# Unread products, own tiles for the first V tails, a later pair of norms and two moves to VectorE, in a kernel of two interleaved attention layers

## The chip, the cores and the metric

The kernel runs on one core of a Trainium2 chip. The metric is the time of one execution on the device, in microseconds. Every kernel is run several times, and the median counts. One execution was also recorded by the hardware profiler; all views quoted here are of that execution. A core has five engines that work side by side: TensorE (PE in the profile; its weight loads are PEld), VectorE (DVE), ScalarE (ACT), GpSimd (POOL) and SyncE (SP), which here only issues transfers. "SPq" and "ACTq" are the issues of transfers by SP and ACT.

## What is computed

Two layers, A and B, are run as A, B, A, B on a sequence of 2048 tokens of width 640. Each adds its result to its input, and each normalises its input first:

```python
x = A_x
x = x + _A_ref(_layernorm(x), ...)
x = x + _B_ref(_layernorm(x), ...)
x = x + _A_ref(_layernorm(x), ...)
x = x + _B_ref(_layernorm(x), ...)
```

Layer A has 32 heads of width 20 and cuts the sequence into 4 segments of 512. Within a segment it is causal softmax attention; it is mixed with a linear attention to a state (M, z) that has summed phi(k) v and phi(k) of the segments before. Layer B has 32 heads of width 128 and goes through 64 segments of 32 tokens one after the other. In each, 8 memory rows and the 32 tokens attend to each other, and the first 8 rows of the result are the memory of the next segment:

```python
for s in range(n_seg):
    h = concatenate([mem, x[s*32:(s+1)*32]])
    q, k, v = h @ Wq, h @ Wk, h @ Wv          # 32 heads of 128
    p = softmax(q k^T * scale, masked)
    o = (p v) @ Wo
    mem = o[:8];  outs.append(o[8:])
```

Inputs, weights and the output are bfloat16.

## The kernel before

**Layer A** (`layer_A`) takes 32 groups of 4 heads in one segment each, 8 per segment, and two more passes of its loop to drain. The first segment's four blocks of 128 rows are loaded, normalised (`seg_norm`) and transposed (`seg_tr`) ahead of the loop; then come the projections of the first group: `proj_q` (tile a_QP), two `proj_kv` (a_KV) and `k_turn` (a_KT). In the loop, `s_mask` puts the causal mask into PSUM by a product of the identity with c_negu, `s_mm` adds the scores (a_S), and `s_max` takes the negative row maxima on VectorE. `q_with_max` adds these maxima to the queries (a_Q), and the copy a_q of that is what the second round of scores needs: `t_round` (a_T) writes transposed scores, three rounds for each pair of heads, `t_exp` applies the exponential on ACT into a_PT, and an affine_select on POOL clears the part above the diagonal. `pv` (a_PV) multiplies with the values, `norm` divides. The pipeline is deep: group g's maxima are taken in pass g, its T rounds come one and a half passes later, its `pv` two passes later. `filler` places one group's projections and copies between the rounds.

After the last pass `last_turns` transposes the normalised rows of the last segment (a_otps), `last_oT` copies them, and `out_stage_b` multiplies them with the output weights (a_YP, two halves of 320 columns for each of four blocks of 128 rows), adds the input on VectorE (a_xnew), stores the sum (xres), makes a bfloat16 copy on ACT (a_xnb, one buffer) and stores that too (xres_bf).

The order of TensorE is the order of the program text. ACT, VectorE and POOL in A are put in order by `KeyOrder`, which sorts instructions by a due time: the step's number plus a lag from `A_LAGS`. SP's order, and all that carries no such rule, is left to the scheduler of the build. PSUM in A is in two pools: three tiles of two banks (psx, for a_S and a_T) and two of one bank (pg, for all else). A tile taken from a pool waits until its predecessor in that buffer was read.

**Layer B** (`layer_B`) is one chain: step s needs the memory rows that step s-1 gave. To keep TensorE's tiles full, what doesn't depend on the memory is computed ahead. Groups of 128 rows are normalised (`ln_norm`, `layernorm_tile`) and transposed (`ln_spread`); the first 24 tokens of each segment go to HX, beside the 8 memory rows, and the last 8 ("tails") of eight segments are gathered in TX. `tail_unit` and `tail_evac` project the tails to queries and keys in 8 units and store them to DRAM (QKd); `vtail_unit` and `vtail_evac` do so with the values in 8 units and store them to VTd. Each step loads its own tails back: `tails_load` (b_tl), `tails_copy`, `vtails_in` (b_Vth).

Ahead of step 0 stand, in the program's text: the loads and norms of four groups, with two spreads; the 8 tail units of the first eight segments, of which the odd k are evicted on VectorE and the even on ACT; the first projections (b_Kp, b_Qp) and their transposes; the loads of the output weights b_wo on SP; the load of the first tails; the 8 V-tail units, evicted by VectorE (even k) and ACT (odd k), stored through SP (even) and ACT (odd); the V rows of the first segment (b_V); `vtails_in(0)`; and one unit of the next eight segments. Each of these evictions needs a place in SBUF. `vt_homes` gives the V tails' places:

```python
vt_homes = [(wk, x) for x in ("vt", "E0", "msb", "PTa", "PTb", "OTsb", "vt", "E0")]
```

so units 6 and 7 write where units 0 and 1 wrote, and unit 5 writes where the last tail unit wrote (its place was `(wk, "OTsb")`). `ps_tile` takes PSUM from a pool of five banks (pp) for nearly all of B.

In B, ACT, VectorE and POOL follow the order of the text too (`_OrdNC`). Between A and B only one thing is fixed: the first norm of B stands on VectorE behind `C.after`, the last instruction of A's last `norm`; the other instructions of A's end and B's start are merged by the scheduler.

Of the kernel before, what the change touches and what calls it, by code (L numbers as in the profile page):

```python
# [37 lines left out]
def alloc_consts(tc, ctx):  # L38
    cp = ctx.enter_context(tc.tile_pool(name="consts", bufs=1))
    C = Consts()  # L40
    C.pool = cp
    C.identb = cp.tile([128, 128], BF16, name="c_identb")
    C.mhalf = cp.tile([128, 1], F32, name="c_mhalf")
    C.negu = cp.tile([128, 2, 128], BF16, name="c_negu")
    C.bdmask = cp.tile([128, 128], F32, name="c_bd")
    C.pad = cp.tile([128, 2, 12], BF16, name="c_pad")
    C.mask12 = cp.tile([128, 12, 40], BF16, name="b_mask12")
# [123 lines left out]
def build_masks(G, C, pool):  # L171

    G.tensor_tensor(out=C.selm[:, 0, :], in0=C.identb[:, 24:32], in1=C.identb[:, 88:96], op=ALU.add)
    G.tensor_tensor(out=C.selm[:, 1, :], in0=C.identb[:, 56:64], in1=C.identb[:, 120:128], op=ALU.add)
    negs = pool.tile([128, 32], F32, name="b_negs", tag="am")
# [22 lines left out]
A_LAGS = {"EK": -1.0, "EKm": 1.05, "EQ": 2.0, "Kn": 0.5, "MZ": 3.5, "MZb": 3.5, "NM1": -0.3, "On": 3.2, "adn":  # L198
# [43 lines left out]
def layer_A(nc, tc, C, W, x_src, x_dst, src_is_bf16, nseg=4, out_bf16=False, xb_dst=None, load_w=None, side_loads=None):  # L242
# [7 lines left out]
    with ExitStack() as ctx:  # L250
# [49 lines left out]

        def seg_load(n_, tt):
# [49 lines left out]
        def out_stage_b(n_, tt, halves=(0, 1)):  # L351
# [11 lines left out]
            for half in halves:  # L363
# [4 lines left out]
                K("xnew").vector.tensor_tensor(out=xnew[:, 320 * half:320 * half + 320], in0=YP[:], in1=xr[:, 320 * half:320 * half + 320], op=ALU.add)  # L368
# [134 lines left out]
        def q_with_max(g):  # L503
# [8 lines left out]
            K("q2").scalar.copy(q2[:], Q2[:])  # L512
# [20 lines left out]
        def t_exp(p, r, Y):  # L533
# [5 lines left out]
            dv = PT[:, :, b:b + 128 * diag].rearrange("p e (a q) -> p e a q", q=128)  # L539
            K("sel").gpsimd.affine_select(out=dv, in_=dv, pattern=[[0, 2], [0, diag], [1, 128]], compare_op=ALU.is_ge,  # L540
# [69 lines left out]
        K.base = None  # L610
        proj_q(0)
# [17 lines left out]
        def item(what, g):  # L629
# [84 lines left out]
        K.close()  # L714
        last_turns(4, NCH)
# [42 lines left out]
def layer_B(nc, tc, C, W, x_src, xb_src, x_dst, mem0, B_Wv, B_Wo, nsteps=64, out_bf16=False, tag=""):  # L758
# [7 lines left out]
    with ExitStack() as ctx:  # L766
# [130 lines left out]
        tail_ps = {}  # L897
# [37 lines left out]
        def vtail_evac(T, k, ps, eng, home=None, dma=nc.sync.dma_start):  # L935
            b4, ch = divmod(k, 2)
            pool_, tg = home or (wk, "vt")
            vt = pool_.tile([128, 256], BF16, name="b_vt", tag=tg)
            evac(eng, vt[:], ps[:])
            for jj in range(2):  # L940
                o = 512 * (2 * b4 + jj) + 256 * ch
                dma(VTd[8 * T:8 * T + 8, :, o:o + 256].rearrange("s t f -> (s t) f"), vt[64 * jj:64 * jj + 64, :])
# [15 lines left out]

        homes = [(bx, "xt"), (bx, "XO"), (bx, "XOd"), (bx, "tl")]
# [12 lines left out]
        for k in range(8):  # L972
            tail_unit(0, k, 0, 8, shared=True)
            tail_evac(0, k, "act" if k % 2 == 0 else "dve", (((kqp, "kq"),) * 4 + ((w2, "QT"), (w2, "KT"), (wk, "tu"), (wk, "OTsb")))[k],
                      (nc.sync if k % 2 else nc.scalar).dma_start)
            if k in (1, 3) and ln_ready:
# [12 lines left out]
        for (nm, b), sb in zip(jobs, sbs):  # L989
            tp = transp4(sb, "b_TP")  # L990
            scatter("dve" if nm == "K" else "act", tp, b, KT[0] if nm == "K" else QT[0], 8, 32, 8 if nm == "K" else 0)
        XO, XOd = init_state()
# [381 lines left out]
```

## Time and profile before

| | |
|---|---|
| median of 3 runs | 2702.46 us (2699.15 to 2707.43) |
| the profiled execution | 2705.0 us, its span 2703.2 us |
| granted TensorE clock, mean | 0.989 |
| PE busy | 2572.6 us (95%) |
| DVE busy | 1693.9 us (63%) |
| ACT busy | 1583.5 us (59%) |
| POOL busy | 709.4 us (26%) |
| DMA | 156.35 MB, mean 58 GB/s |

The first A takes about the first 345 us, the first B goes to about 1351, the second A to about 1697, and the second B to the end. In the order of time a row has its start, its duration from the first to the last of its instructions, the engine, the line, the operation, the tiles written and read and the count; in brackets stand the engine's idle time before and what ended it. Helpers record instructions for others, so most have the line of a helper (L108, L137); the tile's name says what they are.

### The profile page before, as it was taken

Reading aid. Unit: us, or ns where it says so; the run is one execution under the profiler, and the core shown is the slowest. Engines: PE = TensorE matmul, PEld = TensorE weight load, DVE = VectorE, ACT = ScalarE, POOL = GpSimd, SP = SyncE. Lnnn points to the kernel's source line nnn. Section 1 sums busy time; section 2 is a strip of 40 time slices with the busy share of each in tenths; the row PEclk is TensorE's granted clock in tenths of the full one; section 3 lists DMA queues with packets and bytes.
Section 4 is the critical chain, followed back from the end, with each engine's and each line's share of the span. In section 5 each row is a group of like instructions: output and inputs, shape, how many; then the busy total and the mean of one; then the engine's idle time right before and its main releaser. Section 6 shows DMA issues by size and latency. Waiting matters only on the chain. (4 is left out here: it accounts for less than half of the span.)

```text
span 2703.2 us, 146987 instructions
## 1 busy us (share of the span) xinstructions
PE 2572.6 (95%) x65480; PEld 1695.3 (63%) x65480; DVE 1693.9 (63%) x4556; ACT 1583.5 (59%) x3720; POOL 709.4 (26%) x1633
## 2 busy tenths in 40 slices
PE   7999989999999999999989998899999999999998
PEld 4556566666666666666655565566666666666665
DVE  8999845555555555545579998455555555555555
ACT  6988835554545455544369898355545555555543
POOL 5677711111111111111146776011111111111110
PEclk9999989999999999999989999899999999999999
DMA  4122452121222212211220113511111121111110
GB/s 154 47 77 80 146 159 42 42 45 42 45 43 44 44 41 47 43 39 28 74 67 21 60 51 136 164 40 39 40 41 42 42 44 40 42 40 41 37 26 20
DMA packets 326619, 156.35 MB, mean 58 GB/s; under 512 B 246240, under 2 KB 310880, under 8 KB 324192
## 3 DMA queue, kind: packets, MB, share of 16 engines
q1 hardware_dynamic: 316384, 145.38, 21.0%
q8 instruction: 512, 8.39, 1.3%
q10 hardware_dynamic: 9600, 1.57, 0.3%
q14 instruction: 123, 1.01, 0.1%
HBM read 95.15 MB, written 51.71 MB: 54 GB/s over the span
## 5 line engine op out<-in xcount | busy, mean ns | idle before, releaser
L108 PEld LDWEIGHTS <-b_HX 128*32 128x32 bf16 x15360 | 427.2, 97 | 335.8 <-issue 4.6
L108 POOL TENSOR_TENSOR b_Pm<-b_E,b_rs 128x96 bf16<-128x96 bf16 x128 | 63.4, 496 | 1438.0 <-ACT b_Vth L108 1129.4
L137 DVE TENSOR_REDUCE a_nm<-a_S 128x2 f32<-128x512 f32 (+3 forms) x512 | 394.9, 815 | 30.5 <-PE a_S L108 22.6
L137 ACT ACTIVATE a_PT<-a_T 128x1024 bf16<-128x1024 f32 (+1 forms) x384 | 345.1, 903 | 27.1 <-PE a_T L108 19.2
L108 PE MATMUL b_OPS<-b_wo,b_OTsb 128*32 128x320 bf16 x8192 | 306.7, 300 | 8.4 <-issue 6.0
L108 PEld LDWEIGHTS <-b_OTsb 128*32 128x32 bf16 x8192 | 200.3, 96 | 93.6 <-DVE b_OTsb L108 24.3
L108 DVE CAST b_HX<-b_MT 128x8 bf16<-128x8 f32 x372 | 63.7, 172 | 279.9 <-PE b_MT L108 274.8
L137 POOL TENSOR_SCALAR_AFFINE_SELECT a_PT<-a_PT 128x256 bf16<-128x256 bf16 (+1 forms) x384 | 190.2, 504 | 126.2 <-ACT a_PT L137 125.1
L108 ACT CAST b_msb<-b_OPS 128x64 bf16<-128x64 f32 x378 | 69.4, 256 | 235.3 <-PE b_OPS L108 235.3
L108 ACT CAST b_kq<-b_Kb 128x512 bf16<-128x512 f32 x128 | 74.9, 585 | 201.4 <-PE b_Kb L108 201.4
L108 DVE COPY b_KT<-b_TPak 128x128 bf16<-128x128 bf16 x128 | 28.8, 225 | 226.0 <-PE b_TPak L108 226.0
L108 DVE TENSOR_SCALAR b_kq<-b_Qa 128x512 bf16<-128x512 f32 x128 | 88.5, 692 | 116.9 <-PE b_Qa L108 114.0
L108 PE MATMUL b_Ka<-b_wk,b_HX 128*32 128x512 bf16 x2520 | 161.3, 382 | 0.0
L108 PE MATMUL b_Va<-b_wv,b_HX 128*32 128x512 bf16 x2520 | 160.6, 380 | 0.0
L108 PEld LDWEIGHTS <-b_kq 128*128 128x128 bf16 x2080 | 116.9, 98 | 69.3 <-ACT b_kq L108 55.5
L108 PE MATMUL b_Vb<-b_wv,b_HX 128*32 128x512 bf16 x2520 | 160.0, 379 | 0.0
L108 PE MATMUL b_Qa<-b_wq,b_HX 128*32 128x512 bf16 x2520 | 159.2, 380 | 0.0
L108 PE MATMUL b_Qb<-b_wq,b_HX 128*32 128x512 bf16 x2520 | 158.8, 379 | 0.0
L108 PE MATMUL b_Kb<-b_wk,b_HX 128*32 128x512 bf16 x2520 | 158.8, 379 | 0.0
L108 PE MATMUL b_vtail<-b_wv,b_TX 128*32 128x256 bf16 x2880 | 139.3, 273 | 14.3 <-issue 8.6
L108 DVE CAST b_OTsb<-b_OTP 128x160 bf16<-128x160 f32 (+1 forms) x384 | 122.3, 374 | 39.4 <-PE b_OTP L108 39.4
L108 ACT ACTIVATE b_E<-b_SP 128x320 bf16<-128x320 f32 (+1 forms) x256 | 81.0, 368 | 107.9 <-PE b_Va L108 100.2
(204 smaller groups left out, 5774.6 us busy)
## 6 DMA issues: line engine op xcount, KB each, us to landing
b_tl<-b_QKd SPq DMA_DIRECT2D x128, 128.0 KB
b_QKd<-b_tu SPq DMA_DIRECT2D x120, 128.0 KB
b_wv<-in_B_Wv_dram SPq DMA_DIRECT2D x10, 1024.0 KB
b_wo<-in_B_Wo_dram SPq DMA_DIRECT2D x16, 640.0 KB
b_Vth<-b_VTd SPq DMA_DIRECT2D x512, 16.0 KB
b_VTd<-b_vt SPq DMA_DIRECT2D x240, 32.0 KB
b_XO<-xres SPq DMA_DIRECT2D x256, 30.0 KB
xres<-a_xnew SPq DMA_DIRECT2D x19, 320.0 KB
```

Source lines behind the costliest of these rows:

```text
L108: r = f(*a, **k)
L137: r = f(*a, **k)
```

## The change

Six edits.

1. `unread(k)` issues k products of the identity with c_negu, 128 rows by 256 columns, into a tile a_W from pg that nothing reads. They stand ahead of each transposition of the first segment (14, 4, 4, 4 in the first A; 6, 4, 4, 4 in the second), ahead of the first projections (4), behind the last a_Q (4), ahead of every T round of the last two passes (9 times 4), and ahead of the last transposes (10): 80 in the first A, 72 in the second.
2. The copy a_q of the last group is made on VectorE and not on ACT.
3. The selections of the last pair of heads, but for its first round, are made on VectorE as a minimum with c_keep, which holds 3e38 on and above the diagonal and 0 below it.
4. Of B's four first norms, two stand ahead of the tails and two between them: behind units 0 and 2. The third norm is fixed on VectorE behind `C.after2`, A's last sum a_xnew. Their spreads follow units 3 and 5 (before: 1 and 3). `ln_spread` copies TX first, then HX.
5. The V tails' units 0 to 4 get one tile b_vts of 5 x 256 columns, in the buffer of OTsb; units 5 to 7 get PTa, PTb and E0.
6. The last tail unit is evicted into Vth's buffer and not OTsb's.

```diff
+        def unread(k):
+            W_ = pg.tile([128, 256], F32, name="a_W", tag="pg")
+            for _ in range(k):
+                nc.tensor.matmul(W_[:], lhsT=C.identb[:], rhs=C.negu[:].rearrange("p a k -> p (a k)"), start=True, stop=True, skip_group_check=True)
...
-                K("xnew").vector.tensor_tensor(out=xnew[:, 320 * half:320 * half + 320], in0=YP[:], ...
+                C.after2 = K("xnew").vector.tensor_tensor(out=xnew[:, 320 * half:320 * half + 320], in0=YP[:], ...
...
-            K("q2").scalar.copy(q2[:], Q2[:])
+            Z = K("q2")
+            (Z.vector.tensor_copy if g == NGR - 1 else Z.scalar.copy)(q2[:], Q2[:])
...
+            if p == 2 * NGR - 1 and r:
+                K("dsel").vector.tensor_tensor(out=dv, in0=dv, in1=C.keep[:].unsqueeze(1).unsqueeze(1).to_broadcast([128, 2, diag, 128]), op=ALU.min)
+                return
...
             seg_norm(0, tt)
             K.base = None
+            unread((14 if src_is_bf16 else 6, 4, 4, 4)[tt])
             seg_tr(0, tt)
...
+        unread(4)
         proj_q(0)
...
                 q_with_max(g - 1)
+                if g == NGR:
+                    unread(4)
...
+                            if step == 0 and g >= NGR:
+                                unread(4)
                             f = (s_mm, s_max)[step] if kind == "S" else (t_round, t_exp)[step]
...
         K.close()
+        unread(10)
         last_turns(4, NCH)
...
-            if g == 0:
+            if g in (0, 2) and not entered:
...
-                tc.add_manual_dep(f.ins, C.after.ins.name, info, reason="order")
+                tc.add_manual_dep(f.ins, (C.after2 if g else C.after).ins.name, info, reason="order")
...
+            nc.scalar.copy(TX[T][:, :, 4 * half:4 * half + 4, :], tps[:, :, :, 24:32])
             nc.scalar.copy(HX[g][:, :, :, 8:32], tps[:, :, :, 0:24])
-            nc.scalar.copy(TX[T][:, :, 4 * half:4 * half + 4, :], tps[:, :, :, 24:32])
...
+            if isinstance(home, int):
+                if home == 0:
+                    vts[0] = wk.tile([128, 5, 256], BF16, name="b_vts", tag="OTsb")
+                vt = vts[0][:, home, :]
...
-        for g in range(n0):
+        for g in range(2):
             ln_norm(g)
-            if g < 2:
-                ln_spread(ln_ready.pop(0))
+        for g in range(2):
+            ln_spread(ln_ready.pop(0))
...
-            tail_evac(0, k, ..., (... (wk, "tu"), (wk, "OTsb")))[k],
+            tail_evac(0, k, ..., (... (wk, "tu"), (w2, "Vth")))[k],
...
-            if k in (1, 3) and ln_ready:
+            if k in (0, 2) and n0 > 2:
+                ln_norm(2 + k // 2)
+            if k in (3, 5) and ln_ready:
                 ln_spread(ln_ready.pop(0))
...
-        vt_homes = [(wk, x) for x in ("vt", "E0", "msb", "PTa", "PTb", "OTsb", "vt", "E0")]
+        vt_homes = [0, 1, 2, 3, 4] + [(wk, x) for x in ("PTa", "PTb", "E0")]
```

More of the change, by code (lines that the diff above doesn't have):

```diff
@@ L46, in alloc_consts @@
     C.pad = cp.tile([128, 2, 12], BF16, name="c_pad")
+    C.keep = cp.tile([128, 128], BF16, name="c_keep")
     C.mask12 = cp.tile([128, 12, 40], BF16, name="b_mask12")
@@ L174, in build_masks @@
     G.tensor_tensor(out=C.selm[:, 1, :], in0=C.identb[:, 56:64], in1=C.identb[:, 120:128], op=ALU.add)
+    G.memset(C.keep[:], 3e38)
+    G.affine_select(out=C.keep[:], in_=C.keep[:], pattern=[[1, 128]], compare_op=ALU.is_ge, fill=0.0, base=0, channel_multiplier=-1)
     negs = pool.tile([128, 32], F32, name="b_negs", tag="am")
@@ L195 @@
     pass
-A_LAGS = {"EK": -1.0, "EKm": 1.05, "EQ": 2.0, "Kn": 0.5, "MZ": 3.5, "MZb": 3.5, "NM1": -0.3, "On": 3.2, "adn":
+A_LAGS = {"dsel": 0.5, "EK": -1.0, "EKm": 1.05, "EQ": 2.0, "Kn": 0.5, "MZ": 3.5, "MZb": 3.5, "NM1": -0.3, "On": 3.2, "adn":
           2.0, "am": 3.3, "exp0": 0.5, "exp1": 0.2, "exp2": 0.5, "kT": 0.1, "mv": -1.9, "nsb": 0.7, "oT": 0.1,
@@ L367, in out_stage_b @@
                                      start=(c == 0), stop=(c == NCH - 1))
-                K("xnew").vector.tensor_tensor(out=xnew[:, 320 * half:320 * half + 320], in0=YP[:], in1=xr[:, 320 * half:320 * half + 320], op=ALU.add)
+                C.after2 = K("xnew").vector.tensor_tensor(out=xnew[:, 320 * half:320 * half + 320], in0=YP[:], in1=xr[:, 320 * half:320 * half + 320], op=ALU.add)
             if 1 not in halves:
@@ L895, in vtails_in @@
                                   VTd[s].rearrange("t (b n e) -> t n b e", b=2, e=512)[:, j, :, :])
-        tail_ps = {}
+        tail_ps, vts = {}, {}
         def tail_unit(T, k, i0, i1, shared=False):
@@ L936, in vtail_evac @@
             b4, ch = divmod(k, 2)
-            pool_, tg = home or (wk, "vt")
-            vt = pool_.tile([128, 256], BF16, name="b_vt", tag=tg)
-            evac(eng, vt[:], ps[:])
+            if isinstance(home, int):
+                if home == 0:
+                    vts[0] = wk.tile([128, 5, 256], BF16, name="b_vts", tag="OTsb")
+                vt = vts[0][:, home, :]
+            else:
+                pool_, tg = home or (wk, "vt")
+                vt = pool_.tile([128, 256], BF16, name="b_vt", tag=tg)[:]
+            evac(eng, vt, ps[:])
             for jj in range(2):
                 o = 512 * (2 * b4 + jj) + 256 * ch
-                dma(VTd[8 * T:8 * T + 8, :, o:o + 256].rearrange("s t f -> (s t) f"), vt[64 * jj:64 * jj + 64, :])
+                dma(VTd[8 * T:8 * T + 8, :, o:o + 256].rearrange("s t f -> (s t) f"), vt[64 * jj:64 * jj + 64])
         def wo_half(h, jj2):
@@ L957, in o_mm @@
                                          tile_position=(0, 32 * k), skip_group_check=True)
+        entered = []
         homes = [(bx, "xt"), (bx, "XO"), (bx, "XOd"), (bx, "tl")]
@@ L973, in layer_B @@
             tail_unit(0, k, 0, 8, shared=True)
-            tail_evac(0, k, "act" if k % 2 == 0 else "dve", (((kqp, "kq"),) * 4 + ((w2, "QT"), (w2, "KT"), (wk, "tu"), (wk, "OTsb")))[k],
+            tail_evac(0, k, "act" if k % 2 == 0 else "dve", (((kqp, "kq"),) * 4 + ((w2, "QT"), (w2, "KT"), (wk, "tu"), (w2, "Vth")))[k],
                       (nc.sync if k % 2 else nc.scalar).dma_start)
-            if k in (1, 3) and ln_ready:
+            if k in (0, 2) and n0 > 2:
+                ln_norm(2 + k // 2)
+            if k in (3, 5) and ln_ready:
                 ln_spread(ln_ready.pop(0))
@@ L991, in layer_B @@
             scatter("dve" if nm == "K" else "act", tp, b, KT[0] if nm == "K" else QT[0], 8, 32, 8 if nm == "K" else 0)
+        entered.append(1)
         XO, XOd = init_state()
```

## The prediction

> **What bounds the kernel now.** I read the page's slices first. The kernel runs two layers twice, A, B, A, B, and the DVE row shows the seams: A where it stands at 8 or 9, B elsewhere.
>
> ```profile
> span 2703.2 us, 146987 instructions
> PE   7999989999999999999989998899999999999998
> DVE  8999845555555555545579998455555555555555
> PEclk9999989999999999999989999899999999999999
> ```
>
> In B's steps TensorE (PE) is busy throughout, and the change puts nothing on it there. In A's middle VectorE is full, and the change takes nothing off it. What remains are four places: both starts of A, and both ways from A into B, the slices where PE falls to 7 or 8 or PEclk to 8. There I read the stretches, then the order of time. First the end of the first A (columns of a stretch: length, then busy us of PE, weight load, DVE, ACT, POOL, then the granted clock):
>
> ```profile
> 330.00:333.00 3.00, 1.36 (x23) 0.91 (x22) 0.69 (x4) 2.96 (x5) 2.59 (x6) 1.00 0.82 282
> 333.00:336.00 3.00, 2.28 (x47) 1.42 (x44) 1.06 (x4) 3.00 (x5) 3.00 (x7) 0.77 0.92 276
> 342.00:345.00 3.00, 3.00 (x14) 1.69 (x12) 1.70 (x5) 0.37 (x3) 0.55 (x1) 0.52 0.00 0
> ```
>
> After a stretch in which PE was busy 1.36 of 3.00 us its clock is halved, and stays so while PE is the engine that sets the end (3.00 of 3.00 at 342). Inside B's start PE stands almost still for 4 us, and its clock is halved again:
>
> ```profile
> 377.00:379.00 2.00, 0.44 (x10) 0.39 (x10) 0.00 (x0) 0.00 (x0) 0.00 (x0) 1.00 1.07 376
> 379.00:381.00 2.00, 0.01 (x1) 0.03 (x1) 0.00 (x0) 0.00 (x0) 0.00 (x0) 0.50 0.71 226
> ```
>
> **The price of an unread product.** It is 128 by 256, half of a_QP's 512 columns. Five of those take 2.29 us while the clock is low and 1.25 us when it is high:
>
> ```profile
> 1356.61 2.29 PE L108 MATMUL a_QP<-a_xnT,a_wq_pad 128*128 128x512 bf16 x5 [0.78 <-ACT a_xnT L137]
> 1372.44 1.25 PE L108 MATMUL a_QP<-a_xnT,a_wq_pad 128*128 128x512 bf16 x5
> ```
>
> So one unread product costs 2.29/10 = 0.23 or 1.25/10 = 0.125 us, four of them 0.92 or 0.5. There are 80 in the first A and 72 in the second.
>
> **1. Start of the first A: +0.5 us (-1 to +3).** The products need c_negu and stand ahead of the first transposes.
>
> ```profile
> 8.19 0.36 DVE L71 CAST c_negu<-c_neguf 128x128 bf16<-128x128 f32 x2
> 8.96 1.89 PE L108 MATMUL a_tps<-c_identb,a_xn 128*128 128x128 bf16 x15 [8.96 <-DVE a_xn L137]
> 11.80 0.71 PE L108 MATMUL a_tps<-c_identb,a_xn 128*128 128x128 bf16 x5 [0.95 <-DVE a_xn L137]
> 13.29 2.29 PE L108 MATMUL a_QP<-a_xnT,a_wq_pad 128*128 128x512 bf16 x5 [0.78 <-ACT a_xnT L137]
> 15.38 2.42 PE L108 MATMUL a_KV<-a_wkv,a_xnT 128*128 128x160 bf16 x20
> 21.38 0.87 PE L108 MATMUL a_KV<-a_wkv,a_xnT 128*128 128x160 bf16 x10
> ```
>
> Fourteen at low clock are 3.2 us, from 8.55 to 11.8. If the clock is then high, four groups of transposes of half of 0.71 and sixteen products of 0.125 follow, 3.4 us: a_QP could start at 15.2, or 0.4 later if its copy is waited for, 1.9 to 2.3 late. It gains 1.04 us, a_KV 2.42 - 2 x 0.87 = 0.7: net +0.2 to +0.6, and I take 0.5. At low clock to the end of the transposes it is 11.8 + 4 x 0.71 + 16 x 0.23 = 18.3, 5 late; less the gains of 1.74 about +3. A clock high from the seventh product on, 1.5 us sooner, gives -1. I take the value between, since PE has no gap from 8.6 on. (a_QP's 2.29 here is the doubled duration.)
>
> The Trainium skill (TensorE: Matmul & The Clock Gate, Part 1) says that the clock opens only after a whole free-running window of about 3.4 us has been busy. By that rule fourteen products of 0.23 do not fill one window for certain, which speaks for the upper end here, an estimate of +2 us and a total 1.5 us higher. The same section closes the clock after one idle window of that length; the trace does not agree, since the low clock of 334 came with no PE gap over 1.64 us.
>
> **2. Ends of both A: -0.5 us each (-1.5 to +1).** PE, ACT, POOL and DVE hand on to each other here:
>
> ```profile
> 332.03 0.79 PE L108 MATMUL a_T<-a_q,a_kT 32*128 32x512 bf16 x8 [1.64 <-ACT a_q L137]
> 331.85 5.42 ACT L137 ACTIVATE a_PT<-a_T 128x512 bf16<-128x512 f32 x7
> 335.25 2.60 POOL L137 TENSOR_SCALAR_AFFINE_SELECT a_PT<-a_PT 128x512 bf16<-128x512 bf16 x5
> 338.09 1.27 PE L108 MATMUL a_PV<-a_vaug,a_PT 128*128 128x32 bf16 x40
> 340.98 0.61 PE L108 MATMUL a_otps<-c_identb,a_Onat 128*128 128x128 bf16 x4 [1.62 <-DVE a_Onat L137]
> 341.38 3.92 PE L108 MATMUL a_YP<-a_wo,a_oT 128*128 128x320 bf16 x15
> 345.19 0.84 PE L108 MATMUL a_YP<-a_wo,a_oT 128*128 128x320 bf16 x5
> ```
>
> The chain is ACT's exponentials, 331.85 + 5.42 = 337.27, then POOL's selections to 337.85, then a_PV. Moving the query copy frees ACT of what PE waits for at 332.03, and DVE is free by then (0.69 of 3.00 busy). But twelve products now stand ahead of a_Q, in three groups of four, and each group sits ahead of a T round that an exponential waits for: 3 x 0.5 us late on PE, against a gap of 1.64. My walk through it has a_Q end 1.2 us later and the exponentials 0.85 us later. The two selections on DVE give back some 0.2 (0.58 of lag less about 0.4, by 0.52 of a POOL selection below and 0.2 above). a_PV ends 0.4 later. Then the clock: fifteen a_YP at 0.84/5 take 2.52 instead of 3.92, 1.4 less, of which the first two blocks count: 0.9. The ten products after a_PV (1.25) lie in its 1.6 us wait for a_Onat. Bounds: all 36 products' waits uncovered, +1; covered, with the copy's gain, -1.5.
>
> **3. Norms 2 and 3 behind A's last sums: -1 us in the first way (-2 to +0.5), -3.3 in the second (-5 to -1.5).**
>
> ```profile
> 351.82 0.73 ACT L374 CAST a_xnb<-a_xnew 128x640 bf16<-128x640 f32 x1 [1.81 <-DMA xres_bf<-a_xnb]
> 1703.14 0.87 DVE L137 TENSOR_TENSOR a_xnew<-a_YP,a_xr 128x320 f32<-128x320 f32 x2
> 1703.67 2.83 PE L108 MATMUL a_YP<-a_wo,a_oT 128*128 128x320 bf16 x10 [2.48 <-DVE a_xnew L137]
> 1704.09 0.72 ACT L374 CAST a_xnb<-a_xnew 128x640 bf16<-128x640 f32 x1 [5.13 <-DVE a_xnew L137]
> 1707.73 0.59 ACT L108 ACTIVATE b_tu<-b_tail 128x512 bf16<-128x512 f32 x1
> ```
>
> In the second way two sums wait behind two norms on DVE; PE waits 2.48 us for them and then runs ten a_YP at low clock, 2.83 against 1.68. ACT's casts, which stand ahead of the tails' evictions, wait 5.13. With the sums first, the casts run about one per 2.8 us, an estimate (cast 0.73 after a wait of 1.81 for the store of the one before, the row of 351.82 in the first way, so at least 2.5) and b_tu comes at 1705 instead of 1707.73. The norms now stand between DVE's evictions of the tails; PE has four units of tails to cover the first, and I allow 0.4 us of waiting for the second. Sum: 2.5 + 1.15 - 0.4 = 3.3; without the half clock 1.5, with all of the 5.13 us 5. In the first way no such wait shows; its b_tu is held by the casts alone, so about 1 us.
>
> **4. Tiles for the V tails: -3 us in each B (-5 to 0).**
>
> ```profile
> 374.31 0.37 ACT L108 CAST b_vt<-b_vtail 128x256 bf16<-128x256 f32 x1 [2.77 <-DMA b_wo<-in_B_Wo_dram]
> 379.74 1.74 ACTq L108 DMA_DIRECT2D b_VTd<-b_vt  x2
> 382.00 1.26 PE L108 MATMUL b_vtail<-b_wv,b_TX 128*32 128x256 bf16 x20 [2.98 <-ACT b_vt L108]
> 382.20 0.42 DVE L108 CAST b_vt<-b_vtail 128x256 bf16<-128x256 f32 x1 [10.70 <-DMA b_VTd<-b_vt]
> 383.02 2.37 PE L108 MATMUL b_Ka<-b_wk,b_HX 128*32 128x512 bf16 x20
> 386.57 1.26 PE L108 MATMUL b_Kb<-b_wk,b_HX 128*32 128x512 bf16 x20
> 386.91 2.90 SPq L894 DMA_DIRECT2D b_Vth<-b_VTd  x4
> 394.82 0.47 PE L108 MATMUL b_OTP<-b_PTa,b_Vth 32*128 32x40 bf16 x32
> ```
>
> DVE's eviction waits 10.70 us for a store from the same buffer; that wait goes, and one PSUM buffer comes free some 8 us sooner, and with it room for b_vtail, b_Ka and b_Qa in the gap (1.26, 1.26, 1.26 of PE at high clock). ACT's part does not go: it evicts at 374.31 and issues that store only at 379.74. In the built program this store waits for the transfer that used its completion counter before, a b_wo load, in both kernels. So PE is freed for about 3 us of work and stays bound by ACT for the rest. With nothing left of ACT's wait it would be the whole 4 us gap and 1.1 of b_Ka's low clock. What is late next: the V rows of the first step, used at 394.82; their loads are issued at 386.9 to 389.8, and if they only come as early as the stores allow, there are some 3 us in hand.
>
> **5. Start of the second A: -3 us (-5 to -0.5).** Low clock from 1355, with PE busy about half of the time before:
>
> ```profile
> 1352.00:1354.00 2.00, 0.95 (x11) 0.61 (x12) 1.94 (x6) 1.14 (x3) 2.00 (x3) 1.00 0.83 312
> 1354.00:1356.00 2.00, 1.09 (x10) 0.76 (x11) 1.84 (x3) 0.98 (x3) 1.76 (x4) 0.80 0.27 58
> 1360.00:1362.00 2.00, 1.43 (x12) 1.27 (x10) 0.00 (x0) 0.49 (x2) 0.00 (x0) 0.50 1.04 410
> ```
>
> The products lie in PE's waits for DVE (1.05 of 2.00). At high clock a_QP saves 1.04, and of the low stretch that follows, to 1362 in these rows, a_KV and the next a_QP, both at low clock, about 1 each; DVE, idle at 1360, starts its dense stretch by that much earlier. Ends: clock not kept, only the better cover, -0.5; the later low stretch gone too, -5.
>
> **At nothing.** c_keep's two instructions on POOL lie among the masks that only B reads; TX ahead of HX on ACT changes the order of two copies, and the tails, which read TX, come first; the loads of b_XOd move on SP behind the first step's loads, and are read from step 3 on. Without that cover each is one POOL or ACT copy, about 0.5 us.
>
> **Sum.** 0.5 - 2 x 0.5 - 1 - 3.3 - 2 x 3 - 3 = -13.8 us. The profiled execution took 2705.0 us (its span 2703.2 and 1.8 around it): 2691.2. It lies 2.5 above the median 2702.46, so the forecast is 2689.
>
> **Rivals.** (a) *The stores keep the evictions.* ACT's wait for b_wo decides B's start alone, part 4 gives 0: 2689 + 6 = 2695. For it: 379.74 above; against it: the 10.70 us on DVE. 20%. (b) *The clock stays high at all four places* and the V-tail gap closes: the lower bounds of all parts give -1 - 3 - 2 - 5 - 10 - 5 = -26, and half-way between that and -13.8 is -20, which gives 2683. For it: every low-clock stretch follows a half-idle one. 15%. (c) *Slower: the unread products do not raise the clock* and PE, in strict order, pays 0.23 each: 152 x 0.23 = 35 us. Cover is what PE idles there by the rows above: 0.95 + 0.78 at the first start, 1.05 + 0.91 at the second, 1.64 + 0.72 + 1.62 at each end, 11.7 in all: +23, less 6 from part 4 and 4.3 from part 3, +13: 2715. It decides from 45 uncovered products on (10.3 us of gains at 0.23). Against it: a PE that has no gap has full clock everywhere in B. 9%.
>
> **How the numbers follow.** Forecast 56%, its own range 2684 to 2694. No change that can be told is within 0.3%, 8.1 us, so faster means under 2694.4. Most of the forecast (52 of 56) and all of (b) lie below: 0.68, and some of (a): 0.72. Same: rest of (a) and 4: 0.19. Slower: 0.09. The range reaches a little past (b), whose own spread goes further down, and past (a): 2679 to 2701.
>
> **What would show it.** Right: granted clock 1.00 at 334 to 345 and after 1355; no PE wait for a_xnew at 1701; DVE's b_vt evictions without a DMA wait; a_QP of the first start about 2 us later but at 1.25. Wrong: a_W at 0.23 each; ACT's exponentials at A's end over 1 us later; PE still idle 4 us before the second b_Ka, released by ACT; the Vth loads ahead of the first b_OTP.

## The result, and the profile after

| | median (us) | range | runs |
|---|---|---|---|
| before | 2701.40 | 2691.45 to 2711.03 | 22 |
| changed | 2695.97 | 2688.73 to 2701.10 | 22 |

The ratio is 0.998, with a 95% interval of 0.9973 to 0.9988: the change gains 5.4 us (3.2 to 7.3). Twelve further runs, in the experiments below, gave 0.997 (0.9957 to 0.9982), 8 us. The forecast was 13.5 us under the median; the time itself lies near rival (a)'s 2695.

The profiled executions show more than the medians: 2705.0 us before, 2692.1 after, 12.8 apart. From the page of the profile after, the span, the two rows of slices that showed the seams, and the clock:

```profile
span 2690.4 us, 147288 instructions
...
PE   7999989999999999999989999899999999999998
...
DVE  8999845555555555555589998455555555555554
...
PEclk9999999999999999999999999999999999999999
```

The three 8s in PEclk are gone, and where the end of the first A ran at 0.52 (342 to 345, in the prediction) the clock is full:

```profile
342.00:345.00 3.00, 2.49 (x22) 1.61 (x19) 2.66 (x9) 0.77 (x4) 0.55 (x1) 1.00 0.00 0
```

The row of 9s alone does not show that the products did it: two kernels below that have none of them, the one with only the V tiles and the one with only GpSimd's stores, have the same row. Over the whole span the mean granted clock tells more: 0.996 to 0.997 in the four profiles with all the products, 0.988 to 0.994 in the five with none. And part of the 12.8 us lies where nothing was edited. TensorE's waits, grouped by instruction and by what ended them (total us, times, longest), have rows that end with "issue", where nothing in the profile was waited for. Before and after:

```profile
PE b_vtail L108 <- issue: 8.6, 16, 0.7
PE b_OPSd L108 <- issue: 7.0, 8, 2.1
```

```profile
PE b_vtail L109 <- issue: 3.9, 9, 0.7
PE b_OPSd L109 <- issue: 2.1, 6, 0.7
```

Added up, all such rows come to 29.4 us before and 18.2 after. From the first b_OTP to the last group's first sum into b_XOd, the steps of the first B, which the change leaves alone, took 954.4 and 950.6 us. So a single pair of profiles can't place 5 us; below, each stage is read in 14 profiles.

**Where the forecast's signs stand.** Fourteen products at the first start, then the start's own work (start, us, engine, line, operation, output and inputs, shape, count, wait):

```profile
8.62 3.15 PE L109 MATMUL a_W<-c_negu,c_identb 128*128 128x256 bf16 x14 [8.62 <-DVE c_negu L72]
11.96 0.60 PE L109 MATMUL a_W<-c_negu,c_identb 128*128 128x256 bf16 x4
15.05 1.24 PE L109 MATMUL a_QP<-a_xnT,a_wq_pad 128*128 128x512 bf16 x5 [0.34 <-ACT a_xnT L138]
```

As forecast: 0.225 us each, 0.15 later, and a_QP 1.8 us later at 1.24 instead of 2.29. The end of the first A:

```profile
330.41 2.43 ACT L138 ACTIVATE a_PT<-a_T 128x1024 bf16<-128x1024 f32 x3 [1.01 <-PE a_T L109]
331.17 0.61 PE L109 MATMUL a_W<-c_negu,c_identb 128*128 128x256 bf16 x4
332.38 1.25 PE L109 MATMUL a_W<-c_negu,c_identb 128*128 128x256 bf16 x8
334.05 2.43 ACT L138 ACTIVATE a_PT<-a_T 128x1024 bf16<-128x1024 f32 x3 [1.21 <-PE a_T L109]
337.54 2.43 ACT L138 ACTIVATE a_PT<-a_T 128x1024 bf16<-128x1024 f32 x3 [1.06 <-PE a_T L109]
339.97 1.16 PE L109 MATMUL a_PV<-a_vaug,a_PT 128*128 128x32 bf16 x40
```

Before, the last wait of ScalarE for these rounds was this one, and from 331.85 on seven exponentials followed each other without any (5.42 us):

```profile
329.56 1.94 ACT L137 ACTIVATE a_PT<-a_T 128x1024 bf16<-128x1024 f32 x2 [0.38 <-PE a_T L108]
```

So the sign named for "wrong" appears: now ScalarE waits over 1 us for TensorE ahead of each three. The last ends at 339.97 instead of 337.27. The first way into B:

```profile
377.50 0.42 DVE L109 CAST b_vt<-b_vtail 128x256 bf16<-128x256 f32 x1 [1.30 <-PE b_vtail L109]
380.08 1.10 ACTq L109 DMA_DIRECT2D b_VTd<-b_vt  x2
381.23 0.37 ACT L109 CAST b_vt<-b_vtail 128x256 bf16<-128x256 f32 x1 [5.82 <-issue]
381.65 2.32 PE L109 MATMUL b_Ka<-b_wk,b_HX 128*32 128x512 bf16 x20 [4.21 <-ACT b_vt L109]
390.04 0.28 PE L109 MATMUL b_SP<-b_KT,b_QT 128*32 128x40 bf16 x16
395.04 0.47 PE L109 MATMUL b_OTP<-b_PTa,b_Vth 32*128 32x40 bf16 x32
```

VectorE's 10.70 us are gone, and TensorE still stands 4.21 us ahead of b_Ka, for ScalarE, whose store leaves at 380.08 (379.74 before). In the trace's instruction records that store counts its completion on the counter that a b_wo load issued at 371.99 uses too, and it leaves just behind that load's last count, at 380.01 (before: a load issued at 371.24, last count at 379.66). The clock falls here as before, to 0.50 from 380.5 to 387.3, and b_Ka still takes 2.32 us. The first scores stand at 390.04 in both kernels, to the digit. The second start and the second way:

```profile
1353.21 1.24 PE L109 MATMUL a_QP<-a_xnT,a_wq_pad 128*128 128x512 bf16 x5 [0.34 <-ACT a_xnT L138]
```

```profile
1692.50 0.89 DVE L138 TENSOR_TENSOR a_xnew<-a_YP,a_xr 128x320 f32<-128x320 f32 x2 [3.65 <-DMA a_xr<-xres]
1693.04 1.52 PE L109 MATMUL a_YP<-a_wo,a_oT 128*128 128x320 bf16 x10 [1.07 <-DVE a_xnew L138]
1697.04 0.59 ACT L109 ACTIVATE b_tu<-b_tail 128x512 bf16<-128x512 f32 x1
```

a_QP runs at high clock; the sums no longer wait for the norms but for the load of a_xr, and TensorE's wait shrinks from 2.48 to 1.07.

### The profile page after: what moved, and what is told of

It is laid out like the page before. It is cut to its first block, busy times and chain, and to the rows that moved or that the text cites. A ratio compares the mean times of both kernels' runs of the same rounds, so it can differ in the third digit from the quotient of the medians.

```text
span 2690.4 us, 147288 instructions
## 1 busy us (share of the span) xinstructions
PE 2576.7 (96%) x65632; PEld 1699.2 (63%) x65632; DVE 1698.4 (63%) x4562; ACT 1583.1 (59%) x3718; POOL 710.0 (26%) x1631
## 3 DMA queue, kind: packets, MB, share of 16 engines
q1 hardware_dynamic: 316384, 145.38, 21.3%
q14 instruction: 123, 1.01, 0.1%
## 4 chain that ended last, share of the span: by engine, by line
PE 79%; DVE 11%; ACT 5%; DMA 2%; issue 2%; SPq 1%; POOL 0%; ACTq 0%; DVEq 0%; POOLq 0%
PE b_OPS L109 11%; PE b_tail L109 5%; DVE a_nm L138 5%; PE b_Qa L109 5%; PE b_Ka L109 5%; PE b_Kb L109 5%; PE b_Qb L109 5%; PE b_Va L109 5%; PE b_Vb L109 5%; PE b_SP L109 4%; PE b_OTP L109 4%; PE b_OPSd L109 3%; PE b_PTP L109 3%; PE b_vtail L109 3%; ACT a_PT L138 3%; PE a_S L109 2%
## 5 line engine op out<-in xcount | busy, mean ns | idle before, releaser
L109 PEld LDWEIGHTS <-b_HX 128*32 128x32 bf16 x15360 | 427.9, 97 | 343.0 <-issue 12.4
L138 DVE TENSOR_REDUCE a_nm<-a_S 128x2 f32<-128x512 f32 (+3 forms) x512 | 394.9, 815 | 27.6 <-PE a_S L109 20.1
L109 PEld LDWEIGHTS <-b_OTsb 128*32 128x32 bf16 x8192 | 202.0, 97 | 95.7 <-DVE b_OTsb L109 24.3
L138 POOL TENSOR_SCALAR_AFFINE_SELECT a_PT<-a_PT 128x256 bf16<-128x256 bf16 x380 | 188.7, 505 | 128.5 <-ACT a_PT L138 127.2
L109 DVE COPY b_KT<-b_TPak 128x128 bf16<-128x128 bf16 x128 | 28.8, 225 | 228.8 <-PE b_TPak L109 228.8
```

The source lines that it names most:

```text
L109: r = f(*a, **k)
L138: r = f(*a, **k)
```

## The experiments

All were timed beside the kernel before on the same chip, four in a group. The ratios' intervals are some 5 to 9 us wide, so most of what follows goes by stages, each the difference of two starts in the run's timeline. First the expectations on record and the edits, then one table. A ratio here is not the quotient of the two medians beside it; the two differ by up to 0.0012.

**Without the products ahead of the T rounds.**

```
-                if g == NGR:
-                    unread(4)
...
-                            if step == 0 and g >= NGR:
-                                unread(4)
```

> The changed kernel without the unread products ahead of the T rounds and ahead of the last query copy (40 of them in each A); those at both starts of A and the ten after the last a_PV stay. Theory 1 (they delay what they were to help: in the changed kernel the last exponential of the first A ends 2.7 us later than before, at 339.97 instead of 337.27): the last exponential of the first A ends at 337.0 to 337.8 again, and the second A's end gains the same; the clock is low again behind 333 unless the rest suffices, and fifteen a_YP take 3.3 to 3.9 us instead of 2.3. If the exponentials count more, the time is 2 to 4 us under the changed kernel's, ratio to the kernel before 0.9965. Theory 2 (the clock that they keep is worth what they cost): the same time as the changed kernel, ratio 0.998. Theory 3, the forecast's: slower by 1 us for both ends together.

2695.3 against 2704.07, 0.9956. The last exponential ends at 338.64 with the last a_Kn cast 1.4 us later than in the changed kernel's profile, so 2.75 us sooner behind it. From its timeline:

```profile
333.89 4.75 ACT L138 ACTIVATE a_PT<-a_T 128x1024 bf16<-128x1024 f32 x6 [0.26 <-PE a_T L109]
339.74 1.27 PE L109 MATMUL a_PV<-a_vaug,a_PT 128*128 128x32 bf16 x40
340.85 2.29 PE L109 MATMUL a_W<-c_negu,c_identb 128*128 128x256 bf16 x10
```

The stretches (length, then busy us of PE, weight load, DVE, ACT, POOL, granted clock) of the changed kernel, then of this one:

```profile
336.00:339.00 3.00, 3.00 (x48) 1.74 (x44) 1.64 (x4) 1.94 (x3) 1.75 (x4) 1.00 0.68 242
```

```profile
336.00:339.00 3.00, 1.63 (x16) 1.05 (x13) 2.13 (x5) 2.64 (x4) 2.53 (x5) 0.63 0.78 227
```

The clock is low again and the ten products behind a_PV cost 2.29 instead of 1.25. That is cheaper than what held the clock: theory 1.

**V-tail stores of units 5 and 7 on SyncE.**

```
-                       (nc.scalar if k % 2 else nc.sync).dma_start)
+                       (nc.scalar if k in (1, 3) else nc.sync).dma_start)
```

> The changed kernel with the stores of V-tail units 5 and 7 issued by SyncE instead of ScalarE; nothing is left out. Theory 1 (rival (a): ScalarE, held at its store by b_wo's completion counter, is what holds TensorE ahead of the first b_Ka): ScalarE evicts unit 7 by about 376, b_Ka's wait of 4.2 us for it goes in the first way and the 2.0 us in the second, b_Ka and b_Qa run in the gap, and the first scores stand 2 to 4 us earlier in each way, unless the stores, now behind six others on SyncE, bring the V rows too late for the first b_OTP; time 3 to 6 us under the changed kernel's, ratio 0.996 to 0.997. Theory 2 (something else holds the way as well, the b_TX and b_HX copies or the tails' loads): the wait moves to another name, b_SP stays at 390.0, ratio 0.998. Theory 3 (SyncE becomes the bound): b_Vth's loads are issued later than 388 and the first b_OTP comes 1 us or more later than 395.0, ratio over 0.998.

2696.97 against 2704.07, 0.9973. By the stages theories 1 and 3 both hold, and the ratio lies between theirs. First scores 22.0 us behind the first b_Kp instead of 27.7, with no wait ahead of b_Ka, and then the V rows are late:

```profile
386.46 4.92 SPq L966 DMA_DIRECT2D b_VTd<-b_vt  x6
386.73 0.28 PE L109 MATMUL b_SP<-b_KT,b_QT 128*32 128x40 bf16 x16
391.55 3.10 SPq L913 DMA_DIRECT2D b_Vth<-b_VTd  x4
396.14 0.51 PE L109 MATMUL b_OTP<-b_PTa,b_Vth 32*128 32x40 bf16 x32
```

Scores to b_OTP take 9.4 us instead of 5.0: SyncE issues its stores 0.6 to 0.7 us apart, with one pause of 1.9 us, and the loads of the V rows stand behind them.

**Only the V-tail tiles, on the kernel before,** with the change's vtail_evac and the last tail unit in Vth's buffer.

```
-        vt_homes = [(wk, x) for x in ("vt", "E0", "msb", "PTa", "PTb", "OTsb", "vt", "E0")]
+        vt_homes = [0, 1, 2, 3, 4] + [(wk, x) for x in ("PTa", "PTb", "E0")]
```

> The kernel before with only the tiles of their own for the V tails (and the eighth QK tail moved out of their way). The forecast's part 4: 3 us less in each B, b_Ka at 380 instead of 383.0, ratio 0.9978. Rival (a): VectorE's wait of 10.7 us goes, b_vtail unit 6 runs earlier, b_Ka stays at 382 to 383 behind ScalarE, scores at 390.0 as before, ratio 1.000.

2698.44 against 2704.07, 0.9983 (0.997 to 0.9996). In the first way b_Kp to b_OTP is 30.5 us instead of 32.6, in the second 33.3 instead of 32.1. These stages are rival (a)'s. The ratio is nearer to the forecast's 0.9978 than to the rival's 1.000, but the time that it stands for does not lie in the stages that were edited.

```profile
379.94 1.85 ACTq L108 DMA_DIRECT2D b_VTd<-b_vt  x2
382.25 1.26 PE L108 MATMUL b_Ka<-b_wk,b_HX 128*32 128x512 bf16 x20 [1.89 <-ACT b_vt L108]
```

**Only the second start's products, on the kernel before.**

```
+            if not src_is_bf16:
+                unread((6, 4, 4, 4)[tt])
...
+        if not src_is_bf16:
+            unread(4)
```

> The kernel before with only the 22 unread products at the start of the second A. The forecast's part 5: 3 us less (0.5 to 5), ratio 0.9989. Reading of the changed kernel's trace: from the last b_XOd sum to the third a_Kn cast it gained 4.2 us, and 1.2 more by the seventh, 5.3 in all, which would be ratio 0.998, the whole of the change's gain. If that stretch of the kernel before was a bad one by chance, 1 to 2 us.

2698.82 against 2704.07, 0.998 (0.9971 to 0.9989): 5.3 us by the medians, 3.0 to 7.8 by the interval. That is the second reading's 0.998. The stage itself took 311.0 us instead of 317.7, as short as in the best profile of any kernel; but the kernel with only the V tiles, which has no product, came to 311.5. What sets it is the clock (term 5 below).

**The changed kernel once more.**

> The changed kernel itself, beside the others of this group. Ratio 0.998 as before (0.997 to 0.999). Theory 1 (the two profiled executions differ mostly by chance: TensorE waited 29.4 us for instruction issue in the kernel before and 18.2 in the changed one, and A's middle, whose work is the same, took 300.5 us in the first A and 276.3 to 278.9 in the second): the stages with no edit differ from the other profile of the same kernel by up to 3 us each. Theory 2 (they differ by the change): every stage agrees with the first profile of the changed kernel within 0.5 us.

0.997. Theory 1: the second start to the last cast agrees within 1.4 us, but the first B's steps differ by 3.8 and the second B's by 4.5, with the same work.

**No product at all.**

```
-            unread((14 if src_is_bf16 else 6, 4, 4, 4)[tt])
...
-        unread(4)
...
-                    unread(4)
...
-                                unread(4)
...
-        unread(10)
```

> The changed kernel with no unread product at all; V-tail tiles, norms behind the last sums, query copy and selections stay. Theory 1 (products ahead of the T rounds cost 1.7 us in each A by the last a_PV, those at the starts gain 1 to 3 in the second A and nothing in the first): about the changed kernel's time, ratio 0.997 to 0.999. Theory 2 (products are the main gain): ratio 0.9995 or more. Theory 3 (products are a loss as a whole): 3 us or more under the changed kernel, ratio under 0.997.

2701.9 against 2704.53, 0.9989 (0.9977 to 1.0002): all the products together are worth some 6 us beside the changed kernel of the same group, so the rest of the change alone is hardly to be told from nothing. Between theories 1 and 2.

**Only the norms, on the kernel before.**

```
-                tc.add_manual_dep(f.ins, C.after.ins.name, info, reason="order")
+                tc.add_manual_dep(f.ins, (C.after2 if g else C.after).ins.name, info, reason="order")
...
-            if k in (1, 3) and ln_ready:
+            if k in (0, 2) and n0 > 2:
+                ln_norm(2 + k // 2)
+            if k in (3, 5) and ln_ready:
```

> The kernel before with only norms 2 and 3 put behind A's last sums. The forecast's part 3: from the last a_PV to the first b_Kp nothing to 1 us less in the first way (24.1 us before), 3.3 us less in the second (27.4 before, 24.5 in the changed kernel), together ratio 0.9984. Rival: the sums' wait moves to the a_xr loads and to the norms, under 1 us in all, ratio 1.000. Second theory for the V tails: b_wo's loads follow the QK tails' stores on SyncE, so an earlier first b_tu in the second way also brings the second b_Ka earlier by 2 us.

2701.0 against 2704.53, 0.9986. The last a_PV to the first b_Kp: 23.8 us instead of 24.1 in the first way, 25.4 instead of 27.4 in the second. The kernels without this edit lie between 22.2 and 24.4 and between 25.8 and 27.7, so the stages gain little: they are nearer to the rival, though the ratio is near the forecast's 0.9984 (term 3 below). The second theory is not seen: b_Kp to b_OTP stays at 32.8.

**The same stores on GpSimd, without the T rounds' products.** GpSimd's copies of the first tails move behind its stores.

```
-        tails_copy(0, tails_load(0))
+        tl0 = tails_load(0)
...
-                       (nc.scalar if k % 2 else nc.sync).dma_start)
+                       (nc.gpsimd if k in (5, 7) else nc.scalar if k % 2 else nc.sync).dma_start)
+        tails_copy(0, tl0)
```

> The changed kernel without the products ahead of the T rounds and the last query copy, and with the stores of V-tail units 5 and 7 on GpSimd (whose copies of the first tails follow them) instead of ScalarE; nothing is left out. In the run with these stores on SyncE the scores came 5.7 us earlier behind b_Kp (22.0 us instead of 27.7) but the first b_OTP waited 4.5 us for the V rows. Theory 1 (ScalarE's store held the way, and GpSimd's stores, which wait for no completion of b_wo, are early enough): b_Kp to first scores 22 us, scores to b_OTP 5 us, in both ways 3 to 5 us less each, ratio 0.993 to 0.995. Theory 2 (GpSimd's issue is slow): b_QZ's copies or the V rows come late and give it back, ratio 0.996 as without the edit.

2690.63 against 2704.53, 0.9953 (0.9937 to 0.9968). Scores 22.8 us behind b_Kp in the first way and 23.8 in the second, b_OTP 4.8 behind them. The ratio and the stages of the first way are theory 1's; the second way gains little beside the 24.3 of the changed kernel.

**That store edit alone: on the changed kernel, on the kernel before, and with fewer products; and the run above again.** The third, beside what the run above takes out, has no products at the first start:

```
-            unread((14 if src_is_bf16 else 6, 4, 4, 4)[tt])
+            if not src_is_bf16:
+                unread((6, 4, 4, 4)[tt])
```

> The changed kernel with only the stores of V-tail units 5 and 7 on GpSimd; products as changed. If the store behind ScalarE was what kept part 4's gain: first b_Kp to first b_OTP 27.6 us in the first way and 28 to 29 in the second (changed kernel: 29.7 to 32.7 and 29.1 to 31.1), b_Ka with no wait for ScalarE's eviction; the T rounds keep their 22.3 us from the last a_Kn cast to the last a_PV in each A. Time 3 to 6 us under the changed kernel's, ratio 0.995 to 0.996, and 2 to 3 us above the kernel that also drops the T rounds' products.

> The kernel before with only the stores of V-tail units 5 and 7 on GpSimd, no tiles of their own. Theory 1 (two locks in a row: VectorE's eviction of unit 6 waits for the store of unit 0 from the same buffer, ScalarE's of unit 7 for its own store; either alone holds TensorE): VectorE's wait of some 10 us stays, b_Kp to first b_OTP 30.5 to 32.6 us as before, ratio 0.999 to 1.000. Theory 2 (ScalarE's store was the only lock): 27.6 us as with both, ratio 0.996 to 0.997, and the tiles of the change bring nothing.

> The changed kernel with products only at the start of the second A and the ten after the last a_PV, and the stores of units 5 and 7 on GpSimd. The first A starts without products: the first a_Kn cast at 16.6 to 17.5 instead of 17.2 to 18.6 and the first a_q copy at 28.8 to 29.8 instead of 29.5 to 30.7, so 0.6 us under the run that keeps them; ratio 0.993 to 0.996. If the first start's products pay later, by a clock that stays high, 0.5 us or more above it.

> The kernel without the T rounds' products and with the stores of units 5 and 7 on GpSimd once more, beside the others of this group: ratio 0.994 to 0.997. In the first such run the second A's first cast came 15.3 us after the last b_XOd sum instead of 9 to 11, and the first a_Kn to the last took less; if that is chance, 9 to 11 us here and 311 to 314 from the sum to the last cast.

2691.06, 2699.86, 2685.76 and 2686.16 against 2699.17. On the changed kernel the store leaves GpSimd at 376.43 instead of ScalarE at 380.08, and b_Ka follows without a wait:

```profile
376.43 1.88 POOL L109 DMA_DIRECT2D b_VTd<-b_vt  x3 [15.37 <-ACT b_vt L109]
380.70 1.25 PE L109 MATMUL b_Ka<-b_wk,b_HX 128*32 128x512 bf16 x18
387.51 0.28 PE L109 MATMUL b_SP<-b_KT,b_QT 128*32 128x40 bf16 x16
```

On the kernel before the same edit brings nothing, since the other lock, VectorE's wait for its buffer, is still there:

```profile
374.14 1.34 POOL L108 DMA_DIRECT2D b_VTd<-b_vt  x2 [19.23 <-ACT b_vt L108]
381.98 0.43 DVE L108 CAST b_vt<-b_vtail 128x256 bf16<-128x256 f32 x1 [10.25 <-DMA b_VTd<-b_vt]
382.46 2.33 PE L108 MATMUL b_Ka<-b_wk,b_HX 128*32 128x512 bf16 x20 [3.47 <-DVE b_vt L108]
```

TensorE's wait for ScalarE has become one for VectorE, at the same place. The tiles alone gain 2.1 us or lose 1.2, the stores alone nothing, both 4 to 6 us in the first way: two locks, one behind the other. The 15.3 us of the second start in the earlier run were those of its third cast; the first comes 9.2 us behind the last sum, and to the last cast it takes 311.0 us there and 314.0 in the later run.

All 14 profiles by stage (us). "Start 1": the first a_q copy of the first A. "End": start of the last a_Kn cast to start of the last a_PV. "Start 2": last first-half sum into b_XOd of the first B to the last a_Kn cast of the second A, its middle included. "Way 2": last a_PV to first b_Kp. "V": first b_Kp to first b_OTP.

| kernel | median / before | ratio | start 1 | end 1 | V 1 | start 2 | end 2 | way 2 | V 2 |
|---|---|---|---|---|---|---|---|---|---|
| before | | | 29.3 | 20.7 | 32.6 | 317.7 | 20.7 | 27.4 | 32.1 |
| only GpSimd stores | 2699.86 / 2699.17 | 1.0009 | 28.7 | 20.7 | 33.7 | 315.4 | 20.7 | 25.8 | 33.7 |
| only V tiles | 2698.44 / 2704.07 | 0.9983 | 29.6 | 20.7 | 30.5 | 311.5 | 20.7 | 25.8 | 33.3 |
| only start 2 | 2698.82 / 2704.07 | 0.9980 | 29.7 | 20.7 | 32.0 | 311.0 | 20.7 | 27.7 | 32.1 |
| only norms | 2701.00 / 2704.53 | 0.9986 | 28.8 | 21.3 | 33.2 | 315.4 | 20.7 | 25.4 | 32.8 |
| no products | 2701.90 / 2704.53 | 0.9989 | 29.8 | 20.7 | 31.6 | 317.2 | 21.2 | 27.3 | 32.0 |
| changed | 2695.97 / 2701.40 | 0.9980 | 29.5 | 22.3 | 32.7 | 312.5 | 22.3 | 24.5 | 29.1 |
| changed, again | 2695.84 / 2704.53 | 0.9970 | 30.7 | 22.3 | 29.7 | 311.0 | 22.3 | 24.8 | 31.1 |
| SyncE stores | 2696.97 / 2704.07 | 0.9973 | 30.2 | 22.3 | 31.4 | 312.0 | 22.3 | 23.5 | 31.1 |
| GpSimd stores | 2691.06 / 2699.17 | 0.9973 | 29.7 | 22.3 | 28.1 | 313.8 | 22.3 | 23.5 | 27.1 |
| no T products | 2695.30 / 2704.07 | 0.9956 | 29.6 | 20.7 | 32.2 | 313.7 | 20.7 | 23.6 | 29.0 |
| and GpSimd stores | 2690.63 / 2704.53 | 0.9953 | 30.1 | 20.8 | 27.6 | 311.0 | 20.7 | 23.7 | 28.6 |
| the same, again | 2686.16 / 2699.17 | 0.9962 | 29.4 | 20.9 | 27.6 | 314.0 | 20.7 | 22.7 | 30.1 |
| and none at start 1 | 2685.76 / 2699.17 | 0.9959 | 28.8 | 20.7 | 26.4 | 313.2 | 20.7 | 22.5 | 27.6 |

A profiled execution is one of the timed ones and lies up to 7 us off the median (2708.77 against 2701.90 without products), so the stages of a row don't add up to its median.

The last three are faster than both kernels: the first of them stood 5.2 us under the changed kernel in the same group, and 2685.76 us, 13.4 under the kernel before of its group (6.7 to 15.4 by the ratio's interval), is about what the forecast had asked of the change. The last differs from the two above it by less than a measurement tells.

## Why the prediction was wrong

Two steps failed, the overlap in term 2 and the freed time in term 4, and both had their warning in the prediction. Terms 1 and 5 stood, and term 3 in part.

**Term 1, +0.5.** Right: with products the first a_q copy stands at 29.9 on the mean of seven runs, without at 29.2: +0.65. The Trainium skill (TensorE: Matmul & The Clock Gate, Part 1) asks for a whole busy window of about 3.4 us before the clock opens, from which 2 us of loss had been estimated here. The changed kernel's first profile does not show that loss: the fourteen took 3.15 us, the four after them ran at 0.15 each. Its second profile shows part of it: there the four behind the fourteen took 1.06 us, and a_q came at 30.7. In the seven profiles with these products the clock rose 2.9 to 5.1 us after the first of them.

**Term 2, -0.5 for each A.** This step failed. It put "3 x 0.5 us late on PE, against a gap of 1.64", as if the gap were filled once, and had the exponentials 0.85 us late. But ScalarE waits for each round anew, 1.01, 1.21 and 1.06 us in the rows above, 3.3 in all, where it had waited 0.38 and then run seven in a row. Measured: the exponentials 2.5 us later, the last a_PV 1.5 and 1.6 (end 1: 22.3 against 20.8 on the mean of ten; end 2: 22.3 against 20.7). In the second way the clock that they keep is not needed behind a_PV, where the ten products stand: way 2 takes 23.1 us on the mean without the T rounds' products and 24.1 with them. So by the first b_Kp the second end lost some 2.6 us where 0.5 were to be gained. In the first way the clock does count: from the last a_PV to the first b_Kp it is 23.0 us with them (22.4 to 24.4) and 25.5 without (23.7 to 27.2), so that by the first b_Kp nothing is lost there. In the group that ran both, the products ahead of the T rounds cost 4.9 us by the medians (2691.06 against 2686.16) and 3.0 by the ratios, whose intervals overlap. The profiles place some 3 us of that, at the two a_PV; in that pair's profiles the stretch from the last cast to the first b_OTP is not longer with them (73.1 and 72.9 us against 75.8 and 73.5), so where the time is lost in the end stays open. The copy on VectorE shows no gain that can be told: in the five kernels with it and without these products the exponentials end 19.4 to 19.9 us behind the last cast, 19.85 before.

**Term 3, -1 in the first way, -3.3 in the second.** In the second the number is near, the reason holds only in part: 24.1 us on the mean of the four runs with products at both places against 26.7 in the four without norms, -2.6. But norms alone gave 25.4, norms and no product 27.3, and these times go with the clock. It was at 0.50 for 7.2 and 7.3 us of that way in two of the kernels without norms (25.8 us both), for 12.4 and 12.8 in the other two (27.4 and 27.7), and for 7.5 us with the norms alone. So at the same clock the norms gave 0.4 us, although b_tu came 17.7 us behind a_PV instead of 19.6 and 19.7; the forecast had counted the earlier b_tu in full. With the norms and the ten products the clock was low for 2.1 to 3.9 us, with all the products not at all. No run had the ten products without the norms, so how the 2.6 us are to be shared is open. The first gained nothing (b_Kp at 362.36 instead of 362.23), and could not have helped much, because of what follows.

**Term 4, -3 in each B.** This step failed too: it named ScalarE's store as a wait that "does not go", and still counted 3 us of work as freed. The freed unit of b_vtail did run early, and TensorE then stood 4.21 us at the next lock. That lock opens with the loads of b_wo. The changed kernel's second profile shows it, whose first b_Kp came 3.1 us later than in the first:

```profile
365.47 1.26 PE L109 MATMUL b_Kp<-b_wk,b_HX 128*32 128x512 bf16 x20
368.98 5.39 SPq L768 DMA_DIRECT2D b_wo<-in_B_Wo_dram  x5
390.35 0.28 PE L109 MATMUL b_SP<-b_KT,b_QT 128*32 128x40 bf16 x16
```

Its scores stand at 390.35, only 0.3 us later. They follow not b_Kp but the issue of the b_wo loads, which ended at 374.37 (368.98 and 5.39), and at 373.80 in the first. In every profile with the stores on ScalarE, the first scores come 15.3 to 18.4 us after the end of that issue; with the stores elsewhere and the tiles in place 11.0 to 15.0, whatever TensorE did before. So in the first way terms 2, 3 and 4 together, forecast at -4.5, came to nothing: last a_Kn cast to first b_OTP is 77.4 and 76.5 us in the changed kernel's profiles, 77.4 and 74.8 in the two kernels without any edit there. In the second way the V part gained about 2 us (30.1 on the mean of the two profiles, 32.1 without). Why it gained there, where tiles alone gave none (33.3), wasn't tried by itself; the issue of b_wo's loads ends 7.6 and 8.1 us behind b_Kp in the changed kernel and 9.8 to 10.2 in the kernels without the norms, but 9.8 with the norms alone too.

**Term 5, -3.** Right: 312.5 us on the mean of nine runs with products, 315.4 of the five without. The clock is the reason, as forecast. The stage follows the time for which the clock stood at 0.50 in it: not at all in four profiles (311.0 to 311.5 us), 3.4 us in two (312.0 and 312.5), 6.8 in four (313.2 to 314.0), 10.2 in two (315.4 both), 17.1 in two (317.2 and 317.7). With products it was low for 0 to 6.8 us; without them for 10.2 to 17.1 in four profiles, and in the fifth, with only the V tiles, not at all. So the products do not make the best case better, they take the bad ones away, and a single profile without them can look as good.

**The sum** by stages: +0.65, +0.8 (first end and way: 76.9 against 76.1), -3.0, -3.3 (second end and way, last a_Kn cast to first b_OTP: 77.0 against 80.3) is -4.9 us, beside the 5.4 measured; the stages scatter by 1 to 3 us from profile to profile, so that it comes so near is in part luck. The forecast's same four were +0.5, -4.5, -3 and -6.8: what failed is the first way, 5.3 us, and the second, 3.5.

**The rivals.** (a) is what happened in the first way, and its time of 2695 is the nearest; (b) did not come: the clock rose to 0.997 over the whole span, but fell again in the V-tail gap of the first B, which did not close; (c) fell, since the products cost 0.15 once the clock had risen.

## What to carry to other kernels

Work that only keeps a clock up belongs where an engine would wait anyway. Ahead of an instruction that another engine waits for in a loop it was paid here in each round, not once against the sum of the gaps. When a wait is removed, look for the next one at the same instruction before counting the gap as free; where two locks stand in a row, undoing either alone can show next to nothing, and both have to be tried together. An engine that evicts in order should not issue a transfer whose completion counter is still held by a bulk load. And where a stage's time follows the granted clock, compare profiles at the same clock before crediting an edit.

## What the runs showed of the hardware

- GpSimd's stores did not wait for the loads of b_wo: the first left at 374.14, 0.3 us after the eviction at 373.46 had ended, where ScalarE's had left at 379.74.
- TensorE's waits that end with "issue" add up to 18.2 to 29.4 us in the 14 profiles, single ones as long as 2.4 us, at other instructions in each and in no order with the edits. The first B's steps vary by 6.8 us (947.7 to 954.5) and the second's by 7.9 over these profiles, with the same work: so much a single pair of profiles can mislead. The second's take 953.4 to 958.9 us in the five profiles of the kernel before and of single edits on it, 956.2 to 961.3 in the nine of the changed kernel and its variants; whether the edits lengthen them is open.
- Every stretch of low clock in the 14 profiles, but for those at the start and the end of an execution, lasts 3.4, 6.8, 10.2 or 13.7 us: multiples of 3.41.
